# Source order on all five engines in the experts' loop, with a later split of the next x and an earlier first DMA transpose

## The chip, the cores and the metric

The kernel runs on 1 NeuronCore of a Trainium2 chip. The metric is device time in microseconds (us) of one execution, lower is better; the time of a kernel is the median of its runs.

Engine names in the profile: PE is TensorE (PEld its weight loads), DVE is VectorE, ACT is ScalarE, POOL is GpSimd, SP is SyncE. An engine name with a q (SPq, POOLq) is that engine's own instruction queue: DMA issues, semaphores, drains.

## What is computed

Block-sparse attention over 3072 tokens (4 batches of 768, 8 heads of 64), then a top-1 mixture of 8 experts over the attention output. The change touches only the experts.

```python
def _moe_ref(x, modality_id, w_gate, modality_bias, w1, w2):
    N, D = x.shape                      # 3072, 512; w1 is 8 x 512 x 1024, w2 is 8 x 1024 x 512
    logits = x @ w_gate + modality_bias[modality_id]
    e_idx = np.argmax(logits, axis=1)
    ...
    gate_w = probs[np.arange(N), e_idx]
    out = np.zeros((N, D), dtype=np.float32)
    for e in range(E):
        mask = e_idx == e
        h = np.maximum(x[mask] @ w1[e], 0.0)
        out[mask] = gate_w[mask, None] * (h @ w2[e])
    return out
```

## The kernel before

**Stages.** The attention fills roughly the first 230 us. Its rows of x go to a table in device memory (`x_d`), and a routing step sorts the tokens by expert into groups of 256 tokens that share one expert. Groups 0 and 1 are worked early, between the last attention blocks. Groups 2 to 11 are the main loop (`for g in range(NEAR, NG)`, L1456 to L1459), ten times the same body. After it the code branches on the number of groups found (`later`); in this run one half group follows (`half_group`, L1022 and on).

**One group.** Each float32 operand is split into a rounded high part and the remainder as low part, and each product is three matmuls (high by high, high by low, low by high).

- `first_layer(g)`: four steps c (one 1024-column piece of w1 each), in each 24 matmuls of 256 columns (`up`, L809 to L811). They gather four banks `hp`; bank k is complete after the matmuls f = 2k and 2k+1 of step c = 3. Then for each bank `relu` writes the high part of the hidden layer on ACT (L816) and the low part on DVE (L817).
- `second_layer(g)`: four steps k (one piece of w2 each), in each 12 matmuls of 512 columns (`down`, L824 to L826) into two banks `op`. The first matmul of `down` (L824) needs the high part from L816, the third (L826) the low part from L817. `give` then scales the two banks by the gate weight (ACT L841, DVE L843) and scatters the rows to the output from POOL (L845).
- Weights: piece n = 8g + (0 to 7). `ahead(n)`, called at the start of each of the eight steps, calls `fetch(n + 6)`, a 512 KB load from SP (L741 for w1, L745 for w2) into one of 5 staging buffers, and `split(n + 4)`, which casts a staged piece on ACT (L749) and subtracts on DVE (L752; for piece 21 on POOL) into a ring of 5. A split writes over the piece five back, so it waits for PE to be done with that one.
- The next x: `gather(g + 2)` (POOL, L763) fetches 256 rows of x. `apart` (POOL, L786) lays their 32-bit words out as 16-bit halves, `turn_halves` (SP, L790) transposes them by DMA, and `together` (POOL, L796) puts the halves together again. The same function `together` then splits the result: two casts on ACT (L802) and two subtractions on DVE (L803) into `xh` and `xl` of group g + 1. It is called at step k = 0 of `second_layer(g)`.
- Group 11 drains POOL (L982) at its step c = 0, after its gather.

**What sets the order.** In the main loop `tc.manual_schedule(engines={ET.Pool, ET.SP})` keeps POOL and SP in the order of the source; PE, ACT and DVE are ordered by a planner that works with its own estimates. Each engine runs its own list strictly in order: an instruction that waits holds up all that stand behind it on its engine. The attention and the early groups are in source order on all five engines (`MAN`).

The first call of `turn_halves`, for group 3, stands in `first_layer(2)` at step c = 1, after `ahead(17)`. On SP the loads of pieces 22 (issued a second time, the first was in the early groups) and 23 come before it, and on POOL the subtraction of `split(21)`.

Of the kernel before, what the change touches and what calls it, by code (L numbers as in the profile page):

```python
# [9 lines left out]
F32 = mybir.dt.float32  # L10
# [23 lines left out]
NGMAX = NG + E - 1  # L34
NCOL = 2 * NGMAX
TES = (16, 18)
NEAR = len(TES)
# [4 lines left out]
ET = mybir.EngineType  # L42
MAN = {ET.SP, ET.PE, ET.Activation, ET.DVE, ET.Pool}
# [48 lines left out]
def attention_moe(ctx, tc, kD, qD, qH, v0, v1, blocks, modality, w_gate, bias, w1, w2, out):  # L92
# [30 lines left out]
    with ExitStack() as actx:  # L123
# [5 lines left out]
        def bank():  # L129
            return psum.tile([P, 512], F32, name="bank")  # L130
# [546 lines left out]
        stg, wh, wl, xg, xh, xl, hh, hl, og, halves = [], [], [], [], [], [], [], [], [], []  # L677
# [81 lines left out]
        def gather(g):  # L759
            assert all(tau in written for tau in range(TES[g] if g < NEAR else NT))  # L760
            ix = gi_e[g] if g < NEAR else gi[:, 2 * g:2 * g + 2]
            for t in range(2):
                nc.gpsimd.indirect_dma_start(  # L763
                    out=xg[2 * (g % 2) + t], out_offset=None, in_=x_d[0:TES[g] * P] if g < NEAR else x_d,
                    in_offset=bass.IndirectOffsetOnAxis(ap=ix[:, t:t + 1], axis=0))
# [17 lines left out]
        def apart(g):  # L783
            keep_share(g, nc.gpsimd.tensor_copy)
            for t in range(2):
                nc.gpsimd.tensor_copy(halves[0][:, t * GT * 4:(t + 1) * GT * 4].rearrange("p (n f) -> p n f", n=2),  # L786
                                      xg[2 * (g % 2) + t][:, 0:HD].bitcast(U16).rearrange("p (f n) -> p n f", n=2))

        def turn_halves():
            nc.sync.dma_start_transpose(halves[1].rearrange("p (k r) -> p k r", r=P), halves[0])  # L790

        def together(g):
            whole = halves[2].bitcast(F32)
            bits = halves[2].rearrange("p (c t n) -> p n c t", n=2, t=GT)
            for t in range(2):
                nc.gpsimd.tensor_copy(bits[:, :, :, t * P:(t + 1) * P],  # L796
                                      halves[1][:, t * GT * 4:(t + 1) * GT * 4].rearrange("p (n c r) -> p n c r", n=2, c=4))
            for n in range(2):
                h = xh[g % 2][:, 2 * n:2 * n + 2, :].rearrange("p a b -> p (a b)")
                l = xl[g % 2][:, 2 * n:2 * n + 2, :].rearrange("p a b -> p (a b)")  # L800
                x = whole[:, n * 2 * GT:(n + 1) * 2 * GT]
                nc.scalar.copy(h, x)  # L802
                nc.vector.tensor_tensor(l, x, h.bitcast(F32), ALU.subtract)  # L803

        def up(g, c, f, o):
            h, l = wh[(8 * g + c) % NRING], wl[(8 * g + c) % NRING]
            o = o[:, (f % 2) * GT:(f % 2 + 1) * GT]
            fs = slice(f * P, (f + 1) * P)
            nc.tensor.matmul(o, lhsT=h[:, fs], rhs=xh[g % 2][:, c, :], start=c == 0 and f % 2 == 0, stop=False)  # L809
            nc.tensor.matmul(o, lhsT=h[:, fs], rhs=xl[g % 2][:, c, :], start=False, stop=False)  # L810
            nc.tensor.matmul(o, lhsT=l[:, fs], rhs=xh[g % 2][:, c, :], start=False, stop=c == 3 and f % 2 == 1)  # L811

        def relu(k, o):
            rh = hh[0][:, 2 * k:2 * k + 2, :].rearrange("p a b -> p (a b)")
            rl = hl[k // 2][:, k % 2 * 2:k % 2 * 2 + 2, :].rearrange("p a b -> p (a b)")
            nc.scalar.activation(rh, o, AF.Relu)  # L816
            nc.vector.scalar_tensor_tensor(rl, o, 0.0, rh.bitcast(F32), ALU.max, ALU.subtract)  # L817

        def down(g, f, t, o):
            n = 8 * g + 4 + f // 2  # L820
            h, l = wh[n % NRING], wl[n % NRING]
            fs = slice((f % 2) * 512, (f % 2 + 1) * 512)
            ts_ = slice(t * P, (t + 1) * P)
            nc.tensor.matmul(o, lhsT=hh[0][:, f, ts_], rhs=h[:, fs], start=f == 0, stop=False)  # L824
            nc.tensor.matmul(o, lhsT=hh[0][:, f, ts_], rhs=l[:, fs], start=False, stop=False)  # L825
            nc.tensor.matmul(o, lhsT=hl[f // 4][:, f % 4, ts_], rhs=h[:, fs], start=False, stop=f == 7)  # L826
# [11 lines left out]
        def give(g, t, o):  # L838
            w = share[:, g % 4, t:t + 1]
            if t == 0:  # L840
                nc.scalar.mul(og[t], o, w)  # L841
            else:
                nc.vector.tensor_scalar(og[t], o, w, None, ALU.mult)  # L843
            ix = si_e[g] if g < NEAR else si[:, 2 * g:2 * g + 2]
            nc.gpsimd.indirect_dma_start(  # L845
                out=out_t[t], out_offset=bass.IndirectOffsetOnAxis(ap=ix[:, t:t + 1], axis=0),
                in_=og[t], in_offset=None, bounds_check=NTOK - 1, oob_is_err=False)
# [121 lines left out]
        def ahead(n):  # L969
            if n + LOOK_D < 8 * NGMAX:  # L970
                fetch(n + LOOK_D)
            if n + LOOK_S < 8 * NGMAX:
                split(n + LOOK_S)

        def first_layer(g):
            for c in range(4):
                ahead(8 * g + c)
                if c == 0:
                    if g + 2 < NGMAX:
                        gather(g + 2)  # L980
                    if g == NG - 1:
                        nc.gpsimd.drain()  # L982
                if c == 1 and g == NEAR:
                    turn_halves()
                for f in range(8):
                    up(g, c, f, hp[f // 2])
            for k in range(4):
                relu(k, hp[k])

        def second_layer(g):  # L990
            for k in range(4):
                ahead(8 * g + 4 + k)
                for f in (2 * k, 2 * k + 1):
                    for t in range(2):
                        down(g, f, t, op[t])
                if k == 0 and g + 1 < NGMAX:
                    together(g + 1)
                if k == 1 and g + 2 < NGMAX:
                    apart(g + 2)
                if k == 3 and g + 2 < NGMAX:  # L1000
                    turn_halves()
            for t in range(2):
                give(g, t, op[t])
# [252 lines left out]
        for k, it in enumerate(sparse[0] + sparse[1]):  # L1256
            items.append(it)
            if k in DENSE_AFTER:
                c = 2 * DENSE_AFTER.index(k)
# [157 lines left out]
        with man:  # L1417
# [16 lines left out]
            while t < NI + LAG["s"]["G"] + 1 or fillers or slots_todo or choosers or early:  # L1434
                spot = 0
                for op in ORDER:
# [3 lines left out]
                    for kind in "ds":  # L1440
                        k = t - LAG[kind][op]
# [11 lines left out]
                t += 1  # L1453

        hp, op, xp = [bank() for _ in range(4)], [bank() for _ in range(2)], [bank() for _ in range(2)]
        with tc.manual_schedule(engines={ET.Pool, ET.SP}):  # L1456
            for g in range(NEAR, NG):
                first_layer(g)
                second_layer(g)  # L1459
# [3 lines left out]
        def later(g):  # L1463
            if g == NGMAX:
                return
            with tc.If(total > g):
                experts.clear()
                with tc.If(wide <= g) as less:
                    half_group(g)
                with less.Else():  # L1470
                    experts.clear()
                    first_layer(g)
                    second_layer(g)
                    later(g + 1)
# [38 lines left out]
```

## Time and profile before

| | us |
|---|---|
| median of 3 runs | 586.09 |
| lowest, highest | 578.42, 590.53 |
| profiled execution, its time | 584.53 |
| span in its trace, first to last instruction | 582.8 |
| mean granted TensorE clock, as a share of full speed | 0.960 |

The trace covers 582.8 us of the 584.53 us of the profiled execution; the sums of the prediction are made against that execution. In the views a line such as "DVE L752 ... x2 [0.17 <-ACT slot L749]" says that two instructions of source line 752 ran on VectorE, and that the engine sat idle for 0.17 us before them until ScalarE finished line 749. A window row gives, for a stretch of the span, the busy time and number of instructions of each engine, the granted clock, the share of DMA time and the bytes moved.

### The profile page before, as it was taken

What the parts mean: (1) busy time and instruction counts of PE and PEld (TensorE: products, weight loads), DVE (VectorE), ACT (ScalarE), POOL (GpSimd) and SP (SyncE); (2) the same over time, 40 slices, a digit from 0 to 9 for tenths busy, and PEclk for the clock granted to TensorE, in tenths of its full rate; (3) what the DMA queues carried; (4) which work ended last, traced back from release to release, by engine and by line L of the source; (5) the groups of instructions that cost most, each with busy time, mean ns of one, the idle gap of its engine ahead of it and who ended that gap; (6) DMA issues with size and microseconds to landing.
All of it is one profiled execution on the core that took longest, in us unless ns stands there. A gap on an engine that the chain in (4) does not pass through costs nothing.

```text
span 582.8 us, 18937 instructions
## 1 busy us (share of the span) xinstructions
PE 521.9 (90%) x7218; PEld 433.0 (74%) x7218; DVE 381.6 (65%) x1119; ACT 333.0 (57%) x771; POOL 290.5 (50%) x538
## 2 busy tenths in 40 slices
PE   7999998989999988999919897979897998989396
PEld 5677776667777767988917886868796878879285
DVE  6876677677798998598625555454646555554443
ACT  4789868779798885354423544443544444453333
POOL 6597748565588823145830724243451627253313
PEclk9999999999999999999978998989998989999689
DMA  8967978897467886767896685758776686869251
GB/s 310 307 214 205 251 231 219 229 240 210 147 194 214 247 230 181 253 227 244 266 204 183 221 257 184 216 189 248 181 268 181 206 225 225 251 217 270 77 171 32
DMA packets 72341, 125.66 MB, mean 216 GB/s; under 512 B 30641, under 2 KB 30898, under 8 KB 72242
## 3 DMA queue, kind: packets, MB, share of 16 engines
q1 hardware_dynamic: 67984, 110.71, 64.7%
q0 software_dynamic: 4256, 13.65, 7.1%
q8 instruction: 59, 0.97, 0.7%
q14 instruction: 40, 0.33, 0.2%
q10 hardware_dynamic: 2, 0.00, 0.0%
HBM read 105.97 MB, written 12.86 MB: 204 GB/s over the span
## 4 chain that ended last, share of the span: by engine, by line
PE 36%; issue 32%; POOL 12%; DMA 8%; DVE 8%; SPq 2%; ACT 1%; POOLq 0%; another core or an unknown queue 0%; ACTq 0%; DVEq 0%
PE bank L560 6%; DMA slot<-x_d,gi 5%; PE bank L585 5%; POOL at L786 5%; PE bank L616 3%; DMA slot<-v 2%; PE bank L607 2%; POOL out L845 2%; PE bank L826 2%; PE bank L825 2%; PE bank L824 2%; DVE y L568 2%; POOL at L796 2%; PE bank L454 2%; PE bank L633 2%
## 5 line engine op out<-in xcount | busy, mean ns | idle before, releaser
L752 DVE TENSOR_TENSOR slot<-slot 128x1024 fp32r<-128x1024 f32 x99 | 130.4, 1329 | 79.6 <-ACT slot L749 77.9
L749 ACT CAST slot<-slot 128x1024 fp32r<-128x1024 f32 x104 | 107.2, 1047 | 95.8 <-PE bank L826 71.4
L809 PE MATMUL bank<-slot 128*128 128x256 f32 x384 | 108.5, 283 | 0.0
L811 PE MATMUL bank<-slot 128*128 128x256 f32 x384 | 107.9, 281 | 0.0
L810 PE MATMUL bank<-slot 128*128 128x256 f32 x384 | 107.7, 281 | 0.0
L824 PE MATMUL bank<-slot 128*128 128x512 f32 x192 | 82.3, 428 | 26.3 <-ACT slot L816 26.3
L576 ACT ACTIVATE a<-y,mn 128x256 f32<-128x256 f32 x176 | 88.6, 510 | 11.7 <-DVE mn L568 11.5
L826 PE MATMUL bank<-slot 128*128 128x512 f32 x192 | 82.1, 427 | 13.4 <-DVE slot L817 13.4
L845 POOL DMA_INDIRECT out<-slot,si x20 | 25.5, 1276 | 131.6 <-ACT slot L841 128.5
L825 PE MATMUL bank<-slot 128*128 128x512 f32 x192 | 80.9, 421 | 0.0
L809 PEld LDWEIGHTS bank<-slot 128*128 128x128 f32 x384 | 72.3, 188 | 0.6
L810 PEld LDWEIGHTS bank<-slot 128*128 128x128 f32 x384 | 72.2, 188 | 0.4
L811 PEld LDWEIGHTS bank<-slot 128*128 128x128 f32 x384 | 72.3, 188 | 0.0
L824 PEld LDWEIGHTS bank<-slot 128*128 128x128 f32 x192 | 39.5, 205 | 36.8 <-ACT slot L816 28.4
L568 DVE CUSTOM_DVE_ANT_1 y<-bank,smask 128x256 f32<-128x256 f32 x176 | 66.3, 417 | 0.4
L505 POOL COPY slot<-slot 128x128 f32 x264 | 63.7, 293 | 0.0
L530 POOL TENSOR_SCALAR slot<-slot 32x1024 f32<-32x1024 f32 x40 | 41.6, 1041 | 37.2 <-PE bank L616 16.4
L826 PEld LDWEIGHTS bank<-slot 128*128 128x128 f32 x192 | 39.2, 204 | 27.3 <-DVE slot L817 18.3
L590 ACT COPY at<-bank 128x512 f32<-128x512 f32 x88 | 50.6, 576 | 8.3 <-PE bank L585 8.3
L585 PE MATMUL bank<-ident,a 128*128 128x128 f32 x352 | 52.4, 281 | 0.9 <-ACT a L422 0.5
L560 PE MATMUL bank<-slot,q_raw 64*32 64x256 f32 x1408 | 50.1, 382 | 0.9 <-issue 0.9
L803 DVE TENSOR_TENSOR slot<-at,slot 128x512 fp32r<-128x512 f32 x20 | 15.4, 809 | 53.5 <-ACT slot L802 53.5
(313 smaller groups left out, 927.6 us busy)
## 6 DMA issues: line engine op xcount, KB each, us to landing
slot<-w SPq DMA_DIRECT2D x100, 512.0 KB, 4.4
slot<-v SPq DMA_DIRECT2D x180, 128.0 KB, 3.8
x_d<-xr SPq DMA_DIRECT2D x22, 256.5 KB, 4.3
q_raw<-qH SPq DMA_DIRECT2D x22, 256.0 KB, 5.3
slot<-v SPq DMA_DIRECT2D x16, 256.0 KB, 4.7
slot<-kD SPq DMA_DIRECT2D x13, 256.0 KB, 2.9
slot<-v SPq DMA_DIRECT2D x4, 768.0 KB, 9.4
slot<-w SPq DMA_DIRECT2D x10, 256.0 KB, 4.5
```

The lines of the kernel that those rows point to most:

```text
L560: nc.tensor.matmul(sp[u][32 * pr:32 * pr + 32, b * 256:(b + 1) * 256], lhsT=q[r, b * NPAIR + pr, n, :], rhs=kv[r, s0:s0 + 8, b, pr, :], st ...
L568: nc.vector.tensor_tensor_reduce(y[:, u, :].rearrange("p (s f) -> p s f", s=8), sp[u][:, b * 256:(b + 1) * 256].rearrange("p (s f) -> p s ...
L576: nc.scalar.activation(a[:, u, :], y[:, u, :], AF.Exp, bias=mn[:, u:u + 1], scale=-1.0, accum_out=total[:, u:u + 1])
L585: nc.tensor.transpose(tp[:, k:k + P], a[:, u, c * P:(c + 1) * P], ident)
L749: nc.scalar.copy(h, s)
L752: (eng or (nc.gpsimd if n in POOL_SPLITS else nc.vector)).tensor_tensor(l, s, h.bitcast(F32), ALU.subtract)
L809: nc.tensor.matmul(o, lhsT=h[:, fs], rhs=xh[g % 2][:, c, :], start=c == 0 and f % 2 == 0, stop=False)
L810: nc.tensor.matmul(o, lhsT=h[:, fs], rhs=xl[g % 2][:, c, :], start=False, stop=False)
L811: nc.tensor.matmul(o, lhsT=l[:, fs], rhs=xh[g % 2][:, c, :], start=False, stop=c == 3 and f % 2 == 1)
L824: nc.tensor.matmul(o, lhsT=hh[0][:, f, ts_], rhs=h[:, fs], start=f == 0, stop=False)
L825: nc.tensor.matmul(o, lhsT=hh[0][:, f, ts_], rhs=l[:, fs], start=False, stop=False)
L826: nc.tensor.matmul(o, lhsT=hl[f // 4][:, f % 4, ts_], rhs=h[:, fs], start=False, stop=f == 7)
```

## The change

Three edits:

1. The main loop is put in source order on all five engines (`MAN`) in place of POOL and SP alone.
2. `together` keeps only its POOL part (still at k = 0); its ACT and DVE part becomes `halve`, called at k = 2, after that step's `ahead`, so behind `split(8g + 10)` on ACT and DVE.
3. The first `turn_halves` moves from step c = 1 of group 2, behind `ahead(16)` and `ahead(17)`, to the start of that group.

```diff
@@ -790,11 +790,13 @@
         def together(g):
-            whole = halves[2].bitcast(F32)
             bits = halves[2].rearrange("p (c t n) -> p n c t", n=2, t=GT)
             for t in range(2):
                 nc.gpsimd.tensor_copy(bits[:, :, :, t * P:(t + 1) * P],
                                       halves[1][:, t * GT * 4:(t + 1) * GT * 4].rearrange("p (n c r) -> p n c r", n=2, c=4))
+
+        def halve(g):
+            whole = halves[2].bitcast(F32)
             for n in range(2):
                 h = xh[g % 2][:, 2 * n:2 * n + 2, :].rearrange("p a b -> p (a b)")
                 l = xl[g % 2][:, 2 * n:2 * n + 2, :].rearrange("p a b -> p (a b)")
@@ -973,6 +975,8 @@
         def first_layer(g):
+            if g == NEAR:
+                turn_halves()
             for c in range(4):
                 ahead(8 * g + c)
@@ -980,8 +984,6 @@
                     if g == NG - 1:
                         nc.gpsimd.drain()
-                if c == 1 and g == NEAR:
-                    turn_halves()
                 for f in range(8):
                     up(g, c, f, hp[f // 2])
@@ -995,6 +997,8 @@
                 if k == 0 and g + 1 < NGMAX:
                     together(g + 1)
+                if k == 2 and g + 1 < NGMAX:
+                    halve(g + 1)
                 if k == 1 and g + 2 < NGMAX:
                     apart(g + 2)
@@ -1453,7 +1457,7 @@
-        with tc.manual_schedule(engines={ET.Pool, ET.SP}):
+        with tc.manual_schedule(engines=MAN):
             for g in range(NEAR, NG):
                 first_layer(g)
                 second_layer(g)
```

## Rows read from the trace of the kernel before

**Rows 1.** Busy time by stretch, whole core. The columns are the stretch in us, its length, then busy us and count for PE, PEld, DVE, ACT and POOL, the granted clock, the DMA share and GB/s. The first two stretches together are group 2 (from its first up matmul to its last down matmul), then groups 3, 4 and 9, then group 11. Groups 3 to 10, eight of them, fill 319.40 to 528.70.
```profile
281.40:292.90 11.50, 11.50 (x97) 11.29 (x95) 6.08 (x6) 4.19 (x5) 8.45 (x6) 1.00 0.95 221
292.90:319.40 26.50, 13.75 (x48) 10.55 (x48) 10.82 (x11) 8.32 (x12) 5.18 (x6) 0.74 0.73 197
319.40:344.05 24.65, 23.01 (x146) 20.36 (x145) 14.10 (x16) 11.86 (x16) 11.73 (x10) 1.00 0.75 236
344.05:373.10 29.05, 25.95 (x146) 22.53 (x145) 15.62 (x16) 11.91 (x16) 10.67 (x10) 0.88 0.64 203
...
480.00:504.10 24.10, 22.42 (x143) 19.79 (x142) 13.94 (x15) 11.33 (x15) 11.58 (x10) 1.00 0.74 232
...
528.70:564.60 35.90, 26.60 (x147) 22.86 (x147) 15.29 (x16) 12.27 (x16) 9.88 (x10) 0.81 0.55 167
```

**Rows 2.** Who waited for whom from 300 to 550 us: the engine and line that waited, what released it, us in total, times, the longest.
```profile
ACT slot L802 <- POOL at L796: 60.8, 10, 12.4
...
PE bank L824 <- ACT slot L816: 26.3, 10, 11.7
...
PE bank L826 <- DVE slot L817: 12.3, 9, 2.4
```

**Rows 3.** The places where PE sat idle in groups 2, 3, 9 and 11 and the longer one of group 4, from the timeline of PE: start, length, line, and in brackets the idle time before it and what ended it.
```profile
304.58 0.80 PE L824 MATMUL bank<-slot 128*128 128x512 f32 x1 [11.66 <-ACT slot L816]
...
306.89 0.79 PE L826 MATMUL bank<-slot 128*128 128x512 f32 x1 [1.09 <-DVE slot L817]
...
332.02 0.50 PE L824 MATMUL bank<-slot 128*128 128x512 f32 x1 [0.81 <-ACT slot L816]
...
333.59 0.50 PE L826 MATMUL bank<-slot 128*128 128x512 f32 x1 [0.83 <-DVE slot L817]
...
359.75 0.80 PE L826 MATMUL bank<-slot 128*128 128x512 f32 x1 [2.37 <-DVE slot L817]
...
491.94 0.50 PE L824 MATMUL bank<-slot 128*128 128x512 f32 x1 [0.85 <-ACT slot L816]
...
493.50 0.51 PE L826 MATMUL bank<-slot 128*128 128x512 f32 x1 [0.82 <-DVE slot L817]
...
548.73 0.79 PE L824 MATMUL bank<-slot 128*128 128x512 f32 x1 [8.21 <-ACT slot L816]
```

**Rows 4.** The timeline of ACT: piece 22's cast and the split of x in group 2, then the run of instructions around the split of x in group 3 (the split of x, then the casts of pieces 30 and 31, then relu of three banks), then the split of x in group 11.
```profile
288.49 1.05 ACT L749 CAST slot<-slot 128x1024 fp32r<-128x1024 f32 x1 [3.02 <-DMA slot<-w]
301.95 1.14 ACT L802 CAST slot<-at 128x512 fp32r<-128x512 f32 x2 [12.41 <-POOL at L796]
...
328.45 1.14 ACT L802 CAST slot<-at 128x512 fp32r<-128x512 f32 x2 [4.76 <-POOL at L796]
329.49 1.99 ACT L749 CAST slot<-slot 128x1024 fp32r<-128x1024 f32 x2
331.39 1.56 ACT L816 ACTIVATE slot<-bank 128x512 fp32r<-128x512 f32 x3
...
546.10 1.14 ACT L802 CAST slot<-at 128x512 fp32r<-128x512 f32 x2 [10.29 <-POOL at L796]
```

**Rows 5.** The timeline of POOL: `apart` for group 3 at the end of the early groups, `together` in groups 2 and 3, `apart` in groups 3 and 4, `together` in group 11; and from the view of line 982 the one drain (count, duration in ns three times, start).
```profile
279.40 3.01 POOL L786 COPY at<-slot 128x1024 uint16<-128x1024 uint16 x2
...
299.38 2.54 POOL L796 COPY at<-at 128x1024 uint16<-128x1024 uint16 x2 [8.46 <-DMA at<-at]
...
325.78 2.63 POOL L796 COPY at<-at 128x1024 uint16<-128x1024 uint16 x2
...
331.78 3.03 POOL L786 COPY at<-slot 128x1024 uint16<-128x1024 uint16 x2
...
355.00 3.02 POOL L786 COPY at<-slot 128x1024 uint16<-128x1024 uint16 x2
...
543.53 2.54 POOL L796 COPY at<-at 128x1024 uint16<-128x1024 uint16 x2 [8.45 <-issue]
...
L982 POOLq DRAIN  x1: 12527/12527/12527, 530.9 to 530.9; - x1
```

**Rows 6.** The timeline of DVE: the subtractions of two weight pieces and the low parts of relu in group 3, then the subtractions of two weight pieces in group 4.
```profile
330.57 2.36 DVE L752 TENSOR_TENSOR slot<-slot 128x1024 fp32r<-128x1024 f32 x2 [0.17 <-ACT slot L749]
332.85 1.88 DVE L817 SCALAR_TENSOR_TENSOR slot<-bank,slot 128x512 fp32r<-128x512 f32 x3
...
355.19 3.90 DVE L752 TENSOR_TENSOR slot<-slot 128x1024 fp32r<-128x1024 f32 x2 [0.18 <-ACT slot L749]
```

**Rows 7.** SP's queue. The second load of piece 22 and the first transpose from its timeline; all eleven transposes from the view of line 790 (ns, minimum, median, maximum) and their time to landing; what SP waited for; the landing time of the loads of w2 issued at 340 us, just behind the transpose of group 3; and that of the loads of w1 between 260 and 330 us.
```profile
284.44 0.37 SPq L745 DMA_DIRECT2D slot<-w  x1
285.81 5.85 SPq L790 DMA_TRANSPOSE at<-at  x1
...
L790 SPq DMA_TRANSPOSE at<-at x11: 3305/3393/5847, 285.8 to 553.8; - x11
...
DMA to landing us min/median/max: 5.4/6.3/7.3
...
SPq L790 <- POOL slot L752: 5.2, 1, 5.2
...
DMA to landing us min/median/max: 3.9/3.9/3.9
...
DMA to landing us min/median/max: 3.2/8.2/8.8
```

## The prediction

> **What bounds the kernel now.** I read the stretches of the main loop first. PE is the engine to watch: in a calm token group it is busy 23.0 of 24.65 us, while DVE has 14.1, ACT 11.9 and POOL 11.7 [rows 1]. But the groups do not take the same time. Group 2 takes 11.5 + 26.5 = 38.0 us, groups 3 to 10 together 528.7 - 319.4 = 209.3 us, from 24.1 to 29.05 each, and group 11 takes 35.9 us [rows 1]. The slow ones also show a granted clock below 1: 0.74, 0.88, 0.81 [rows 1].
>
> Then the waits. PE waits in two places only, both at the seam from the first to the second layer: the first down matmul waits for relu's high part (26.3 us in all, one of 11.7), the third for its low part (12.3 us) [rows 2]. The timeline of PE places them: 11.66 + 1.09 us in group 2, 8.21 in group 11, 0.8 + 0.8 in groups 3 and 9, and 2.37 for the low part in group 4 [rows 3].
>
> Then why relu is late. ACT's list, as the planner made it, has the split of the next x (L802) ahead of the casts of pieces 8g + 6 and 8g + 7 and ahead of relu. L802 waits for POOL's `together`: ten times, 60.8 us in all [rows 2]. In group 3 ACT stands still for 4.76 us until 328.45 with the cast of piece 30 behind it, which could have run before; the two casts and relu then come at 329.49 and 331.39, and PE starts at 332.02 [rows 3, 4]. In group 2 `together` waits for the first transpose until 299.38, so ACT stands for 12.41 us [rows 4, 5]; in group 11 it waits behind the drain (12.5 us long) until 543.53, and ACT stands for 10.29 us [rows 4, 5]. So the bound is a list, not a resource: a thing needed in the next group stands ahead of a thing needed now.
>
> **What a calm group takes without its waits.** Group 3: 24.65 - 0.81 - 0.83 = 23.0 us; group 9: 24.1 - 0.85 - 0.82 = 22.4 us [rows 1, 3]. I take 22.8 us, eight steps of 2.85 us, with t = 0 at the first up matmul.
>
> **Source order, groups 3 to 10.** The last cast before relu (piece 8g + 7) waits for PE to end step c = 2, at t = 8.6. A cast takes 1.0 us (1.99 for two), relu 0.5 to 0.6 (1.56 for three) [rows 4], so the cast ends near 9.75 and the first relu near 10.3. PE wants it at 11.4: no wait. On DVE a subtraction takes 1.2 us and a low part 0.63 (2.36 for two, 1.88 for three) [rows 6]: subtraction 9.8 to 11.0, first low part to 11.65. The third down matmul is due at 11.4 + 0.46 = 11.85: no wait, but only 0.2 us to spare. What can use that up is POOL. In group 4 `apart` began at 355.00 and the two subtractions beside it took 3.90 us in place of 2.36, which made the wait 2.37 [rows 3, 5, 6]. In the new order the subtraction of 8g + 6 runs beside `together` (6.2 to 9 us into the group, 325.78 - 319.4 and its length [rows 1, 5]) and may cost 1.54 us more: it would end near 9.7, as the next is due. `apart` begins 11 to 12.4 us into a group (355.00 - 344.05, 331.78 - 319.4 [rows 1, 5]), beside the low parts. Those ran at full speed beside it in group 3 (from 332.85, `apart` from 331.78 for 3.03 us) [rows 5, 6]. Bounds of what remains: 0 and 2.4 us a group; I take 0.4, nearest to the rows of group 3. So 23.2 x 8 = 185.6 us in place of 209.3: **23.7 us less**. This counts the clock as full, as it was in groups 3 and 9; group 4's loss of clock came with the longer wait [rows 1, 3].
>
> [...]
>
> **The later split of x.** At k = 2 it stands behind the cast of 8g + 10, which waits for the end of step k = 1 (t = 17.1). Casts and subtractions of x then end near 18.1 + 1.14 + 1.3 = 20.6 (two casts of x take 1.14 us [rows 4]; the subtractions about as long). The next group wants them at 22.8: 2.2 us to spare, so nothing on the path. `together` ends 9 us into a calm group, 8 us before. In group 11 it ends at 543.53 + 2.54 - 528.7 = 17.4 [rows 1, 5], just before the cast of 8g + 10 does (18.1). So the drain is hidden behind six steps of PE work, by 0.7 us only; if the drain grew, every us past that would hold ACT.
>
> **Group 11.** Its 8.21 us and the loss of clock beside it go: 22.8 + 0.4, and I add 0.8 for the register loads and the branch after the loop, which now stand behind the last instructions of the list on every engine (bounds 0 and 2). 24.0 in place of 35.9: **11.9 us less**.
>
> **The earlier transpose, group 2.** The first transpose is issued at 285.81 and takes 5.85 us against a median of 3.39, and the waits of SP put 5.2 us of waiting at it to POOL's subtraction of a weight piece [rows 7], which in the source stands just ahead (piece 21). At the head of the group it has neither that nor the two loads before it. Its own input was ready at 279.40 + 3.01 = 282.4 (POOL's `apart` for group 3) [rows 5]. So I expect issue 282.5 to 285.8 and landing 5.4 to 7.3 us later [rows 7], 291.2 to 293.1, in place of 299.38, when `together` could start [rows 5].
>
> It costs the loads. Piece 22 was issued at 284.44 [rows 7] and ACT waited for it until 288.49 [rows 4]; now it goes at 285.9 and piece 23 at 286.9. Under source order their casts stand ahead of relu, so relu waits for them. Lower bound: they land as the loads just behind the transpose of group 3 did, in 3.9 us [rows 7], 289.8 and 290.8; then cast, subtractions and first low part end near 294.7 and PE, ready at 293.0, waits 1.3 us in all. Upper bound: they land behind the transpose, near 294.4 and 295.7; the low part is then ready at 298.8, a wait of 5.4 us, and a loss of clock beside it as in group 4, up to 3.4. I take 4.5 us in all, nearer to the row. 22.8 + 4.5 = 27.3 in place of 38.0: **10.7 us less**.
>
> [...]
>
> **The sum.** 23.7 + 11.9 + 10.7 = 46.3 us from the profiled execution's 584.53: 538.2. That execution is 1.6 us below the median of the runs shown, 586.09, so **540 us**. If every wait and every loss of clock went, the loop would take 10 x 22.8 = 228 us in place of 283.2, so 55 us is the most there is: 531 us.
>
> **The rivals.**
> 1. As forecast, 540 us, own range 531 to 549. Chance 0.66.
> 2. DVE takes the place of ACT: subtractions that meet POOL keep the third down matmul waiting about 2.4 us in every second group, with the clock falling as in group 4 (29.05 - 24.65 = 4.4 us more [rows 1]). Four such groups: 17.6 us, 557 us. For it: 0.2 us to spare. Against it: the low parts at full speed beside `apart`. Chance 0.16.
> 3. The stall of group 2 turns into a wait for the loads at the upper bound, and the drain of group 11 runs past k = 2 by some us: 4.3 + 4, 548 us. Chance 0.07.
> 4. The later split does not do what it says: its wait only moves to the next group's start. It needs `together` to end 11 us later than in group 3, or the split to take 2.2 us more than I worked out; at 3 us over in all ten groups the seam would be free but the group start not, with the clock falling: 10 x 3 + 8 = 38 us given back, 578 us. Against it: 8 us of room. Chance 0.06.
> 5. Slower: the loads. In source order a late load of piece 8g + 7 holds ACT and so relu, one to one, with no freedom left to the planner. That piece is issued just behind the transpose, from 340 us in group 3, and lands in 3.9 us [rows 7]; group 4 would want it at 319.4 + 23.2 + 8.6 = 351.2, 7 us after landing. To end slower by over 2% (598 us) the loop would have to give back 58 us, 6 us a group, so landings of some 17 us; the longest among the loads of w1 around here is 8.8 [rows 7], and the DMA share is 0.75 in a calm group [rows 1] (0.8 at 23.2 us). Chance 0.05.
>
> **The numbers.** Cases 1, 2 and 3 are faster by over 2% (below 574.4; 2% is about what a measurement of this kernel can tell from no change, since its runs shown spread from 578.4 to 590.5): 0.89. Case 4 is within 2%: 0.06. Case 5: 0.05. For eight times in ten the range goes from the least that is possible, 531, to just past case 2: 558.
>
> **What would show it.** Right: PE's wait for L816 near zero in groups 3 to 10 and 11; L802 behind relu and with hardly any wait on POOL; calm groups of 22.8 to 23.5 us at a clock of 1.00; the first transpose issued near 282.5 without its 5.2 us. Wrong in the step of group 2: casts of pieces 22 and 23 after 294. Wrong in the step of DVE: the wait of L826 for L817 still above 1 us in several groups. Wrong in the step of the split: ACT waiting at L802 in group 11, or up matmuls (L809, L810) waiting for L802 or L803 at a group's start.

## The result: 0.92 of the time before

| | median us | lowest to highest | runs | ratio to before, 95% interval |
|---|---|---|---|---|
| before | 588.31 | 578.42 to 592.35 | 4 | |
| changed | 535.37 | 533.40 to 537.49 | 4 | 0.9195 (0.9070 to 0.9321) |

The forecast was 540 us, with 531 to 558 as its range. All ratios in this document compare undisturbed runs only (e1 has just one, and so no ratio), so a median can lie a little off its ratio.

The profile of the changed kernel has a span of 532.3 us and a mean clock of 0.988 (0.960 before). Lines after 790 are shifted by two: relu is L818 and L819, `down` L826 to L828, `up` L811 to L813, the split of x L804 and L805, `together` L795. The same stretches as in [rows 1]: group 2, group 3, groups 4 to 10, group 11, the half group.

```profile
276.21:306.47 30.26, 25.40 (x146) 21.98 (x144) 19.12 (x17) 12.78 (x17) 13.62 (x12) 0.89 0.84 261
306.47:328.94 22.47, 22.47 (x146) 20.38 (x145) 15.74 (x15) 12.29 (x16) 9.69 (x10) 1.00 0.80 246
328.94:486.38 157.44, 157.44 (x1010) 142.53 (x1008) 109.82 (x105) 86.07 (x106) 76.23 (x70) 1.00 0.82 257
486.38:508.87 22.49, 22.49 (x145) 20.40 (x144) 14.70 (x15) 12.28 (x16) 11.76 (x10) 1.00 0.61 197
508.87:532.30 23.43, 14.43 (x81) 12.55 (x79) 8.21 (x10) 6.83 (x10) 6.67 (x5) 0.88 0.36 103
```

From the second row to the fourth PE is busy for the whole stretch at a clock of 1.00: nine groups in 202.4 us, 22.5 each, where eight took 209.3 and group 11 alone 35.9 before [rows 1]. What still loses is at the two ends: group 2 (30.26 us at 0.89) and the half group (23.43 us at 0.88). Group 2 takes 7.8 us more than the 22.47 of group 3: 4.08 + 0.77 us are waits (next view), and the other 2.9 are longer matmuls, 25.40 us of busy PE in place of 22.47, with the lower clock.

All places from 276 us on where PE sat idle before a matmul, from its timeline:

```profile
291.79 0.80 PE L826 MATMUL bank<-slot 128*128 128x512 f32 x1 [4.08 <-ACT slot L818]
293.78 0.79 PE L828 MATMUL bank<-slot 128*128 128x512 f32 x1 [0.77 <-DVE slot L819]
...
518.24 0.39 PE L1013 MATMUL bank<-slot 128*128 128x256 f32 x1 [3.16 <-ACT slot L1035]
```

Of the 10 + 9 waits at the seams before [rows 2] two are left, both in group 2, and the half group has a new one. And ACT around the seam of group 3, answering to [rows 4]: casts, four relus, then, at k = 2, the split of x without any wait.

```profile
315.07 1.05 ACT L749 CAST slot<-slot 128x1024 fp32r<-128x1024 f32 x1 [1.77 <-PE bank L812]
316.03 2.59 ACT L818 ACTIVATE slot<-bank 128x512 fp32r<-128x512 f32 x4
...
323.57 1.05 ACT L749 CAST slot<-slot 128x1024 fp32r<-128x1024 f32 x1 [1.72 <-PE bank L828]
324.53 1.14 ACT L804 CAST slot<-at 128x512 fp32r<-128x512 f32 x2
```

**Where the 50.5 us between the two spans lie.** From the starts of the groups on PE's timeline (before, after, difference):

| | before | after | difference | forecast |
|---|---|---|---|---|
| ahead of group 2 | 281.42 | 276.21 | -5.2 | 0 |
| group 2 | 38.28 | 30.26 | -8.0 | -10.7 |
| groups 3 to 10 | 209.29 | 179.91 | -29.4 | -23.7 |
| group 11 | 35.59 | 22.49 | -13.1 | -11.9 |
| half group | 18.22 | 23.43 | +5.2 | 0 |
| sum | 582.80 | 532.30 | -50.5 | -46.3 |

The first line is not the change: up to the loop the instruction lists of the engines are the same, and in the runs below that have the same lists the loop begins anywhere from 276.2 to 287.6 us (e10). So the experiments are read by what follows that stage as well: the time from the first `give` of group 1 on ACT, just ahead of the loop, to the end of the span.

| run | median us | ratio (95%) | first give at | from there | group 2 | group 3 | group 11 | half group |
|---|---|---|---|---|---|---|---|---|
| before | 588.31 | 1 | 280.91 | 301.9 | 38.28 | 24.66 | 35.59 | 18.22 |
| changed | 535.37 | 0.9195 (0.907 to 0.932) | 275.70 | 256.6 | 30.26 | 22.47 | 22.49 | 23.43 |
| e1 | 538.68 | none given | 280.71 | 256.5 | 23.42 | 31.18 | 22.50 | 21.45 |
| e2 | 584.86 | 1.0105 (0.991 to 1.030) | 280.31 | 300.2 | 38.41 | 24.66 | 34.07 | 18.54 |
| e3 | 577.10 | 0.9905 (0.983 to 0.998) | 277.65 | 295.0 | 30.45 | 26.21 | 34.25 | 18.73 |
| e4 | 537.48 | 0.9348 (0.921 to 0.948) | 279.93 | 254.1 | 23.71 | 25.87 | 22.50 | 24.03 |
| e5 | 586.69 | 1.0135 (1.008 to 1.020) | 284.00 | 300.2 | 38.19 | 24.65 | 34.99 | 18.49 |
| e6 (changed) | 541.72 | 0.9336 (0.928 to 0.939) | 283.77 | 256.4 | 29.97 | 22.46 | 22.50 | 23.53 |
| e7 | 533.91 | 0.9238 (0.919 to 0.929) | 279.10 | 252.6 | 31.02 | 22.46 | 22.49 | 18.68 |
| e8 | 531.41 | 0.9179 (0.912 to 0.924) | 282.91 | 251.7 | 30.19 | 22.47 | 22.50 | 18.60 |
| e9 | 527.42 | 0.9027 (0.899 to 0.906) | 279.78 | 245.7 | 23.48 | 22.46 | 22.49 | 19.35 |
| e10 | 529.12 | 0.9011 (0.895 to 0.907) | 287.08 | 246.2 | 24.60 | 22.46 | 22.50 | 18.72 |
| e11 (changed) | 540.62 | 0.9254 (0.921 to 0.930) | 279.50 | 258.6 | 29.31 | 22.47 | 22.50 | 26.35 |

e1 to e4, e5 to e8 and e9 to e11 each ran side by side on one chip with the kernel before.

### The profile page after: what moved, and what is told of

Its sections match the earlier page's. It is cut to its first block, busy times and chain, and to the rows that moved or that the text cites. A ratio compares the mean times of both kernels' runs of the same rounds, so it can differ in the third digit from the quotient of the medians.

```text
span 532.3 us, 18937 instructions
## 1 busy us (share of the span) xinstructions
PE 505.2 (95%) x7218; PEld 427.0 (80%) x7218; DVE 389.2 (73%) x1119; ACT 336.1 (63%) x771; POOL 288.2 (54%) x538
## 4 chain that ended last, share of the span: by engine, by line
PE 78%; DVE 8%; DMA 5%; issue 3%; ACT 2%; SPq 2%; POOL 1%; POOLq 0%; another core or an unknown queue 0%; ACTq 0%; DVEq 0%
PE bank L828 9%; PE bank L827 8%; PE bank L826 8%; PE bank L811 8%; PE bank L813 8%; PE bank L812 8%; PE bank L560 6%; PE bank L585 6%; PE bank L616 3%; PE bank L607 3%; PE bank L454 2%; PE bank L633 2%; DMA slot<-w 2%; PE bank L432 2%; DVE y L568 2%
## 5 line engine op out<-in xcount | busy, mean ns | idle before, releaser
L752 DVE TENSOR_TENSOR slot<-slot 128x1024 fp32r<-128x1024 f32 x99 | 142.1, 1446 | 73.5 <-ACT slot L749 72.7
L811 PE MATMUL bank<-slot 128*128 128x256 f32 x384 | 108.5, 283 | 0.0
L813 PE MATMUL bank<-slot 128*128 128x256 f32 x384 | 107.9, 281 | 0.0
L826 PE MATMUL bank<-slot 128*128 128x512 f32 x192 | 76.9, 401 | 4.1 <-ACT slot L818 4.1
L828 PE MATMUL bank<-slot 128*128 128x512 f32 x192 | 76.7, 400 | 0.8 <-DVE slot L819 0.8
L827 PE MATMUL bank<-slot 128*128 128x512 f32 x192 | 76.9, 400 | 0.0
L811 PEld LDWEIGHTS bank<-slot 128*128 128x128 f32 x384 | 72.3, 188 | 0.6
L812 PEld LDWEIGHTS bank<-slot 128*128 128x128 f32 x384 | 72.2, 188 | 0.4
L813 PEld LDWEIGHTS bank<-slot 128*128 128x128 f32 x384 | 72.3, 188 | 0.0
L560 PE MATMUL bank<-slot,q_raw 64*32 64x256 f32 x1408 | 48.7, 382 | 0.0
L826 PEld LDWEIGHTS bank<-slot 128*128 128x128 f32 x192 | 36.7, 191 | 12.2 <-ACT slot L818 4.3
L828 PEld LDWEIGHTS bank<-slot 128*128 128x128 f32 x192 | 36.6, 191 | 10.0 <-DVE slot L819 1.5
L827 PEld LDWEIGHTS bank<-slot 128*128 128x128 f32 x192 | 36.6, 191 | 8.4 <-DVE slot L752 0.4
## 6 DMA issues: line engine op xcount, KB each, us to landing
x_d<-xr SPq DMA_DIRECT2D x22, 256.5 KB, 4.4
```

The costliest lines, as they stand in the source:

```text
L560: nc.tensor.matmul(sp[u][32 * pr:32 * pr + 32, b * 256:(b + 1) * 256], lhsT=q[r, b * NPAIR + pr, n, :], rhs=kv[r, s0:s0 + 8, b, pr, :], st ...
L752: (eng or (nc.gpsimd if n in POOL_SPLITS else nc.vector)).tensor_tensor(l, s, h.bitcast(F32), ALU.subtract)
```

## The experiments

### e1: edit 1 alone

```diff
-        with tc.manual_schedule(engines={ET.Pool, ET.SP}):
+        with tc.manual_schedule(engines=MAN):
```

> Edit 1 alone: source order on all five engines, the split of x still at k = 0, the first transpose still behind the two loads. Theory (a list: the split of x stood ahead of relu): behind relu at k = 0 it holds nobody at the seam, groups 3 to 10 take 22.5 us as in the changed kernel, PE's waits at the seam are near zero; in groups 2 and 11 ACT stands at the split (8 and 5 us) but the casts behind it are wanted only in the next group; total 532 to 541. Rival (the three edits are needed together): the split at k = 0 waits for the late transpose in group 2 and for the drain in group 11 and PE waits over 5 us at the start of groups 3 and of the half group; total 545 to 555.

538.68 us (530.29 to 543.13), 256.5 us from the first give in its one profile: as good as all three edits together (256.4 to 258.6 in three profiles). The lists of PE, POOL and SP are the same as before, instruction for instruction; only ACT's and DVE's differ, and only in the loop. So source order on PE is worth nothing here, and the whole of it lies in two lists. The waits of PE, though, have moved to group 3:

```profile
293.82 0.50 PE L826 MATMUL bank<-slot 128*128 128x512 f32 x1 [0.63 <-DVE slot L817]
...
305.39 0.39 PE L810 MATMUL bank<-slot 128*128 128x256 f32 x1 [0.47 <-DVE slot L803]
...
321.33 0.80 PE L824 MATMUL bank<-slot 128*128 128x512 f32 x1 [4.44 <-ACT slot L816]
```

Group 2 is short (23.42) and group 3 long (31.18). On ACT's timeline the split of x, ready at 303.75, stands ahead of three casts that run only then; their staging buffers come free late, the loads for group 3 with them, and the cast that relu of group 3 stands behind waits 6.95 us for a weight piece. So the theory's "wanted only in the next group" left out the loads that wait for those casts. The rival's wait at the start of group 3 was there with 0.47 us, not 5.

### e2: edit 2 alone

```diff
+                if k == 2 and g + 1 < NGMAX:
+                    halve(g + 1)          # together() without its ACT and DVE part, planner order as before
```

> Edit 2 alone: the planner orders PE, ACT and DVE, the split of x is written at k = 2. Theory: what counts is only where the split of x stands; if the planner leaves it behind relu, total 533 to 545, with casts of pieces 8g + 6 and 8g + 7 in time; if it pulls it ahead of relu again, no change, 578 to 592. Rival (source order itself brings the gain): above 560 with the split behind relu.

584.86 us, ratio 1.0105 (0.991 to 1.030): no gain, and 300.2 us from the first give, 1.7 less than before. The planner pulled the split ahead of the casts and relu again, as ACT's timeline in group 3 shows:

```profile
322.15 1.05 ACT L749 CAST slot<-slot 128x1024 fp32r<-128x1024 f32 x1 [1.68 <-PE bank L812]
327.98 1.15 ACT L804 CAST slot<-at 128x512 fp32r<-128x512 f32 x2 [4.78 <-POOL at L795]
329.02 1.99 ACT L749 CAST slot<-slot 128x1024 fp32r<-128x1024 f32 x2
330.92 1.56 ACT L818 ACTIVATE slot<-bank 128x512 fp32r<-128x512 f32 x3
```

This is the condition that the expectation named for no change, so this run alone doesn't tell theory from rival. It tells that the later place in the source did nothing here, since the planner orders ACT by itself.

### e3: edit 3 alone

```diff
+            if g == NEAR:
+                turn_halves()
             for c in range(4):
                 ahead(8 * g + c)
-                if c == 1 and g == NEAR:
-                    turn_halves()
```

> Edit 3 alone: the first transpose ahead of the two loads, all else as before. Theory: ACT's wait at the split of x in group 2 falls from 12.4 us to 3 to 5, PE's wait there from 12.75 to 4 to 6, groups 3 to 11 as before; 7 to 10 us less than before, 575 to 582. Rival (the loads behind the transpose give it all back): within 2 us of before.

577.10 us, ratio 0.9905 (0.983 to 0.998); 6.9 us less from the first give. Group 2 falls from 38.28 to 30.45, with PE waiting 3.25 + 2.36 us; groups 3 to 11 wait as before. That is just under the 7 to 10 us of the theory. Under the planner's list the early transpose is a gain, because ACT stood waiting for it (12.41 us at the split of x in group 2 before [rows 4], 2.60 here).

### e4: edits 1 and 2 without edit 3

Against the changed kernel:

```diff
-            if g == NEAR:
-                turn_halves()
             for c in range(4):
                 ahead(8 * g + c)
+                if c == 1 and g == NEAR:
+                    turn_halves()
```

> Edits 1 and 2 without edit 3 (the first transpose behind the two loads as before). Theory: in the changed kernel the 4.9 us that PE waits in group 2 come from piece 23, loaded behind the transpose; without edit 3 that wait is under 1 us, the split of x waits for POOL's together at k = 2 by some 2 us, group 2 takes 24 to 27 us in place of 30.0; total 529 to 535. Rival (the early transpose is needed): the split of x comes too late for group 3, group 2 takes 31 us or more; total 536 to 542.

537.48 us, 254.1 from the first give, 2.5 us less than the changed kernel's profile. Group 2 takes 23.71 us in place of 30.26. So under source order edit 3 is a loss in group 2 of 6.5 us. Group 3 gives 3.4 us of it back (25.87): PE waits 1.98 us for the split of x at its start, the rival's mechanism in small, and 0.89 at its seam. The total is over the theory's 529 to 535; the loop is within it, the stage ahead of the loop began later than in the changed kernel's profile.

### e5: source order, with the split of x where the planner had it

```diff
+                if c == 2 and g + 1 < NGMAX:
+                    halve(g + 1)
                 ahead(8 * g + c)
...
+                if c == 1 and g + 1 < NGMAX:
+                    together(g + 1)
                 for f in range(8):
                     up(g, c, f, hp[f // 2])
...
-        with tc.manual_schedule(engines={ET.Pool, ET.SP}):
+        with tc.manual_schedule(engines=MAN):
```

> Source order on all five engines, but the split of the next x (ACT and DVE) written where the planner had put it: at c = 2 of the first layer, ahead of the casts of pieces 8g + 6 and 8g + 7 and of relu; the first transpose behind the two loads as in the kernel before. From the first give (of group 1) to the end the kernel before takes 301.9 us, the changed one 256.6 and edit 1 alone 256.5. Theory (the place of the split is the whole matter): 295 to 303 us from there to the end, PE waits 0.8 + 0.8 us or more at each seam, total 577 to 590. Rival (other parts of the planner's list, as its cast of 8g + 8 ahead of the fourth relu, cost as well): half or more of the gain stays, under 280 us from there to the end, total under 565.

586.69 us, ratio 1.0135 (1.008 to 1.020), 300.2 from the first give, and the waits of the kernel before are back at every seam. In groups 2, 3 and 11:

```profile
307.24 0.80 PE L826 MATMUL bank<-slot 128*128 128x512 f32 x1 [11.23 <-ACT slot L818]
...
335.02 0.50 PE L826 MATMUL bank<-slot 128*128 128x512 f32 x1 [0.81 <-ACT slot L818]
336.58 0.50 PE L828 MATMUL bank<-slot 128*128 128x512 f32 x1 [0.83 <-DVE slot L819]
...
550.86 0.80 PE L826 MATMUL bank<-slot 128*128 128x512 f32 x1 [8.62 <-ACT slot L818]
```

Source order on every engine with this one thing in the old place is as slow as the kernel before. The lists of PE, POOL and SP are those of e1 and of the kernel before, though `together` is written earlier; e1 and e5 differ in the lists of ACT and DVE alone. So the gain is the place of the split of x, behind the last two casts and relu, and nothing else of the planner's list. This is the run that settles it.

### e6 and e11: the changed kernel again

> The changed kernel once more, as the measure for the two runs beside it: 533 to 538 us, and 255 to 258 us from the first give of group 1 to the end of the trace.

> The changed kernel beside the two: 533 to 542 us, and 255 to 258 us from the first give of group 1 to the end.

541.72 and 540.62 us; the first is above the 533 to 538 expected of it. The ratios are 0.9336 and 0.9254 beside 0.9195. From the first give 256.4 and 258.6 (255 to 258 were expected), beside 256.6 in the first profile. In e6 the difference in total is ahead of the loop (first give at 283.77, not 275.70). In e11 3.8 of the 5.8 us between the two profiles are (279.50), and its half group is 2.9 us longer (26.35).

### e7: no transpose for a group that is not there

`turn_halves` and `apart` of group 13 stand in group 11 for a full group 12, which these inputs don't have.

```diff
-                if k == 1 and g + 2 < NGMAX:
+                if k == 1 and g + 2 < NGMAX and g != NG - 1:
                     apart(g + 2)
-                if k == 3 and g + 2 < NGMAX:
+                if k == 3 and g + 2 < NGMAX and g != NG - 1:
                     turn_halves()
...
                 with less.Else():
                     experts.clear()
+                    if g == NG:
+                        apart(g + 1)
+                        turn_halves()
                     first_layer(g)
```

> The changed kernel, but group 11 leaves out apart and the transpose of the x of group 13, and the branch for a full group 12 makes them itself (not taken with these inputs). Theory (the half group's last two weight pieces wait on SP behind that transpose, which waits for POOL behind the drain): the half group falls from 23.7 to about 18.2 us, 5 us less than the changed kernel beside it. Rival (those loads are late because DMA is busy or their staging buffers come free late): at most 1.5 us less.

533.91 us beside e6's 541.72; the half group takes 18.68 us, not 23.53, and PE waits nowhere in it. In the changed kernel's trace the chain reads so (POOL, SP twice, ACT):

```profile
504.45 3.02 POOL L786 COPY at<-slot 128x1024 uint16<-128x1024 uint16 x2
...
507.50 1.83 SPq L790 DMA_TRANSPOSE at<-at  x1
512.41 1.11 SPq L745 DMA_DIRECT2D slot<-w  x2
...
516.66 1.04 ACT L749 CAST slot<-slot 128x1024 fp32r<-128x1024 f32 x1 [3.21 <-DMA slot<-w]
```

`apart`, behind the drain, ends at 507.47; the transpose waits for it; the last two weight pieces wait on SP behind the transpose, and behind the register loads that follow the loop (3.1 us from the transpose's end to the first of the two loads), and the half group waits for them. Before, group 11 took 13 us longer, and the same chain was hidden in that. The theory is right: 4.9 us of the half group, 3.8 of the time from the first give.

### e8: no second load of piece 22

On top of e7:

```diff
-            if n + LOOK_D < 8 * NGMAX:
+            if 8 * NEAR + 6 < n + LOOK_D < 8 * NGMAX:
                 fetch(n + LOOK_D)
```

> As e7, and piece 22 is no longer loaded a second time at the start of group 2, so that only piece 23 is loaded behind the first transpose. Theory (in group 2 relu waits for piece 23, which waits its turn behind the transpose and the second load of piece 22): PE's wait in group 2 falls from 4.9 us to 0 to 2, group 2 from 30.0 to 23 to 26 us; another 4 to 6 us less than e7. Rival (the transpose itself holds piece 23 up): PE still waits 3 us or more, at most 2 us less than e7.

531.41 us; 0.9 us less than e7 from the first give, not 4 to 6; group 2 30.19 us. The time is the rival's, but not by the rival's cause. The theory's wait is gone, PE no longer waits for relu's high part, and group 2 is as long as ever: a wait of 5.44 us for the low part has taken its place. The two subtractions ahead of the low parts (DVE's timeline first, with the first subtraction alone and then both, then POOL's):

```profile
290.26 8.77 DVE L752 TENSOR_TENSOR slot<-slot 128x1024 fp32r<-128x1024 f32 x1 [2.92 <-ACT slot L749]
...
290.26 9.91 DVE L752 TENSOR_TENSOR slot<-slot 128x1024 fp32r<-128x1024 f32 x2 [2.92 <-ACT slot L749]
300.09 2.47 DVE L819 SCALAR_TENSOR_TENSOR slot<-bank,slot 128x512 fp32r<-128x512 f32 x4
...
290.81 2.43 POOL L752 TENSOR_TENSOR slot<-slot 128x1024 fp32r<-128x1024 f32 x1
293.15 2.64 POOL L795 COPY at<-at 128x1024 uint16<-128x1024 uint16 x2
295.68 0.32 POOL L781 COPY share<-slot 128x1 f32<-128x1 f32 x2
295.92 2.02 POOL L786 COPY at<-slot 128x1024 uint16<-128x1024 uint16 x2
```

2.36 us of work [rows 6] took 9.91 while POOL ran one instruction after another from 290.81 to 297.94. The first subtraction alone took 8.77 of it and ended at 299.03, 1.1 us after POOL's run; the second then took 1.2. So the early transpose costs group 2 in two ways, either of which is enough: the load behind it, and POOL's copies, which come earlier with it and fall beside the two subtractions. In the changed kernel the first hid most of the second (the subtractions took 6.56 us there).

### e9: e8 with the first transpose back behind the loads

The edit of e4 on top of e8, which itself stands on e7.

> As e8 (no transpose and no apart for group 13 in group 11, no second load of piece 22), but the first transpose back behind the loads (edit 3 undone). From the first give of group 1 to the end e8 took 251.7 us, e7 252.6, the changed kernel 256.6, edits 1 and 2 alone 254.1 with 3.5 us of waiting in the half group. Theory (POOL's copies then run after the two subtractions of group 2, not beside them): 249 to 251 us from there to the end, PE waits under 1 us at the seam of group 2 and 0 to 2 at the start of group 3; total 526 to 533 by how long the stage ahead of the loop takes. Rival (the early transpose is worth its place): 253 us or more.

527.42 us, ratio 0.9027 (0.899 to 0.906); the changed kernel beside it had 0.9254 (0.921 to 0.930), and the intervals don't meet. 245.7 us from the first give, better than the 249 to 251 expected. PE has one wait left in the loop, 0.70 us in group 2, and none at the start of group 3, where e4 had 1.98: the second load of piece 22, which stood ahead of the transpose there, is left out, and the split of x is in time. This and e10 are the fastest versions found.

### e10: e8 with two subtractions behind relu

```diff
-                split(n + LOOK_S)
+                split(n + LOOK_S, rest=lows_ if n + LOOK_S in (8 * NEAR + 6, 8 * NEAR + 7) else None)
...
             for k in range(4):
                 relu(k, hp[k])
+            while lows_:
+                lows_.pop(0)()
```

> As e8, but in group 2 DVE's subtractions of pieces 22 and 23 stand behind the four low parts of relu. Theory (in e8 those two subtractions took 9.91 us beside POOL's run of subtraction, together and apart, and the low parts, which POOL does not slow, stood behind them): PE's wait of 5.44 us at the third down matmul of group 2 falls under 0.5, group 2 from 30.2 to 23 to 24 us, 244 to 247 us from the first give to the end, total 522 to 530. Rival (the low parts are held up by POOL too, or the late subtractions then hold up the down matmuls of pieces 22 and 23): PE waits 3 us or more in group 2, at most 2 us less than e8.

529.12 us, 246.2 from the first give, 5.5 less than e8; group 2 24.60, not 23 to 24. (The profiled execution took 535.04 us; the stage ahead of its loop was the longest of all.) The wait for the low part is gone. One of 1.57 us is left, on the high part, since the cast of piece 23 waited 4.67 us for its load. The low parts ran beside `apart` at full speed (DVE, then POOL):

```profile
300.63 2.48 DVE L819 SCALAR_TENSOR_TENSOR slot<-bank,slot 128x512 fp32r<-128x512 f32 x4 [9.07 <-ACT slot L818]
...
300.25 2.01 POOL L786 COPY at<-slot 128x1024 uint16<-128x1024 uint16 x2
```

So what POOL held up in e8 were the subtractions, and the low parts only because they stood behind them.

## Why the prediction was right

- **The list.** Right, and shown by e1 and e5: the split of x ahead of relu on ACT and DVE was what the change cured. Its place alone is worth 43.7 us from the first give (e5 300.2, e1 256.5), the changed kernel's gain 45.3. It was not all that the loop lost: e9 is 10.9 us better still.
- **Groups 3 to 10.** Forecast 23.2 us each, measured 22.5; the 0.4 us kept for subtractions that meet POOL did not come, and 0.3 of the calm group's 22.8 was not there either. The subtractions did meet `together`, at the forecast price and more: 4.05 us for two in place of 2.36 (first line below, group 3), ending just as the low parts began, and PE never waited.

```profile
313.33 4.05 DVE L752 TENSOR_TENSOR slot<-slot 128x1024 fp32r<-128x1024 f32 x2 [1.63 <-ACT slot L749]
317.30 2.48 DVE L819 SCALAR_TENSOR_TENSOR slot<-bank,slot 128x512 fp32r<-128x512 f32 x4
```

- **Group 11.** Forecast 24.0, measured 22.5. The 0.8 us for the register loads behind the loop was an estimate that no row gave, and no run shows it on PE in group 11; on SP they lie in the chain of e7. `together` ended at 500.42 + 3.88 = 504.3 and the split began at 504.48: the drain was hidden by a margin of 0.2 us, thinner than the 0.7 forecast, as the copies took 3.88 us rather than 2.54.
- **Group 2.** Forecast 27.3, measured 30.26, near the upper bound, 22.8 + 5.4 + 3.4 = 31.6. The transpose itself went as forecast: issued 1.6 us into the group, without the long wait (2.20 us in place of 5.85 [rows 7]). The step that failed is the price of the loads behind it. I took 4.5 us in all, near the row of a load that landed in 3.9 us behind group 3's transpose [rows 7]; PE's waits alone were 4.85, and the clock added 2.9. Here the two loads, issued at 280.17 and 281.53, had ACT waiting until 285.48 and 290.19, 5.3 and 8.7 us. The sign that the prediction set for this step, casts after 294, is 288.8 on this profile's clock, and the cast of piece 23 is past it. The landings of the loads of w1 in that stretch, 8.2 us in the median [rows 7], would have been the nearer row:

```profile
277.76 2.20 SPq L790 DMA_TRANSPOSE at<-at  x1
...
285.48 1.05 ACT L749 CAST slot<-slot 128x1024 fp32r<-128x1024 f32 x1 [5.23 <-DMA slot<-w]
290.19 1.04 ACT L749 CAST slot<-slot 128x1024 fp32r<-128x1024 f32 x1 [3.66 <-DMA slot<-w]
```

  In e4, where they go ahead of the transpose, piece 23 made nobody wait, and group 2 took 23.71 us: the edit that was counted as a help for group 2 cost it 6.5. The upper bound lay nearer; that it had the two loads land behind the transpose, near 294.4 and 295.7 (289.2 and 290.5 on this profile's clock), was my estimate and stood in no row, and the casts began at 285.48 and 290.19. Without the second load of piece 22, piece 23 still took 5.4 us (e8, issued at 287.19, cast at 292.55) and 7.3 (e10, issued at 291.75, cast at 299.05). So that load is a part of the 8.7; how the rest divides between the transpose and all that the DMA engines moved then (share 0.95 in that stretch before [rows 1]) no run shows.

  The prediction also added the 5.4 to 7.3 us of [rows 7], which count from the start of the issue, to its end: 282.5 gives 287.9 to 289.8, not 291.2 to 293.1. In the changed kernel `together` started 8.4 us after the issue, at 286.16, straight behind POOL's subtraction, and what POOL's copies then do to the subtractions of pieces 22 and 23 was not in the sum.
- **The second rival was there, in one place.** DVE held up by POOL was given 0.16 as a cost of every second group. It cost nothing in those groups and 0.8 us in group 2. There more of it lay hidden behind the loads: e8, with one of them gone, shows 5.4 us of waiting.
- **The half group.** Taken as unchanged; it lost 5.2 us. The step that failed is not a price but a place not looked at: what group 11's long stall had hidden. A transpose that nobody reads stood ahead of the last two loads on SP, and when the stall went it came to light (e7).
- **Luck in the total.** 535.4 against 540 forecast looks like 4.6 us; in the two later sessions the same kernel had 541.7 and 540.6. The stage ahead of the loop varied by 11 us between profiles with the same lists. Taken by the loop and what follows it, the forecast was -46.3 us and the first profile shows -45.3 (the -50.5 of the table without the -5.2 ahead of the loop). That closeness is made of four misses: groups 3 to 10 gave 5.7 us more than forecast (29.4, not 23.7) and group 11 1.2 more (13.1, not 11.9), while group 2 gave 2.7 less (8.0, not 10.7) and the half group lost 5.2 that were not forecast.

**Open:** what makes the stage ahead of the loop begin the loop anywhere from 276.2 to 287.6 us was not tried. Nor was the drain's length (12.5 us before [rows 5]). One execution of each run was profiled, and one kernel had 256.4 to 258.6 us from the first give; so differences of 2 us there say little.

## What to carry to other kernels

When an engine's list shows a wait for something that only a later stage needs, look at what stands behind it: here the price was that of the things behind, two casts and relu behind a wait of 4.76 us in group 3 [rows 4], and moving the one instruction brought 43.7 us (e1, e5), while the planner put it back when only its place in the source was changed (e2). When a stall goes, list what ran under it, each queue in turn, to the end of the kernel: here 5 us of a useless transpose came up in the tail (e7). And the transfer that was moved forward here moved the loads behind it back (piece 22 was issued 4.0 us into group 2, not 3.0 [rows 7]), and brought forward the copies that wait for it (`together` began 10.0 us into the group, not 18.0 [rows 5]): group 2 took 30.26 us with the move and 23.71 without (e4). Each of these needs its own look at what then runs beside it.

## What the runs showed of the hardware

- An instruction that waited held up what stood behind it on its engine. On ACT two casts and relu stood behind the split of x, 4.76 us in group 3 [rows 4]; on DVE the low parts stood behind two subtractions of 9.91 us (e8), on SP two loads behind the transpose that waited for `apart` until 507.47 (the chain at e7), and on POOL `together` of group 11 behind the drain of 12.5 us [rows 5].
- A DVE subtraction of two operands in SBUF, 1.2 us alone (two take 2.36 [rows 6]), was not done before a run of POOL instructions had ended, in two places. In e8 one that met a run of 7.1 us took 8.77. In the changed kernel one that began 2.7 us into a run of the same length (283.83 to 290.91) took 5.43. Both ended 1.1 us after POOL's run; in e10, begun at 303.03 behind POOL's run (to 302.26), four of them took 4.62. The lines of the changed kernel (DVE, then POOL):

```profile
286.56 5.43 DVE L752 TENSOR_TENSOR slot<-slot 128x1024 fp32r<-128x1024 f32 x1 [6.21 <-ACT slot L749]
...
283.83 2.41 POOL L752 TENSOR_TENSOR slot<-slot 128x1024 fp32r<-128x1024 f32 x1
286.16 2.60 POOL L795 COPY at<-at 128x1024 uint16<-128x1024 uint16 x2
288.66 0.31 POOL L781 COPY share<-slot 128x1 f32<-128x1 f32 x2
288.90 2.01 POOL L786 COPY at<-slot 128x1024 uint16<-128x1024 uint16 x2
```

  It is not always so: in group 4 before, the first of two subtractions took 1.92 us and ended 0.9 us before `apart` did. The low parts, with one operand in a PSUM bank, were not slowed beside the same copies (2.48 us for four in e10 beside `apart`, 2.47 in group 2 of the changed kernel with POOL still). What it is in POOL's instructions that holds up the one and not the other no run shows. That a subtraction of 1.2 us could last as long as a whole run on POOL is what I had not expected.
- A load of 512 KB issued just behind the first transpose and another such load was usable 8.5 to 9.2 us after its issue (four profiles: the changed kernel's three and e7), 5.4 and 7.3 us without that other load (e8, e10), where one behind a later transpose landed in 3.9 [rows 7].
- In the nine groups without a wait the granted clock was 1.00 in each of the three stretches that they make up (second to fourth row of the first view). Before, it was 1.00 in groups 3 and 9 too, with waits of 0.8 + 0.8 us at the seam [rows 1, 3], and waits of 0.74 + 2.37 us in group 4 came with 0.88 over the group. But group 8 had the short waits, 0.78 + 0.83 us, and a clock of 0.93 over its 26.16 us:

```profile
453.48:479.64 26.16, 24.55 (x145) 21.49 (x144) 14.10 (x15) 11.86 (x16) 11.63 (x10) 0.93 0.75 216
```

  So the prediction's reading, that the loss of clock came with the longer wait, holds for groups 3, 4 and 9 and not for group 8.
